# A three-stage attention and mixture-of-experts kernel: a fixed order of the last tiles and of slot 0 on all engines, kinds of slots read a slot ahead, waits per half of weights, two k pairs in most first loops

## The chip, the cores and the metric

The kernel runs on one core of one Trainium2 chip. The metric is the device time of one execution in microseconds (us); a median of three runs is given. A difference within 0.2% is about what a measurement of this kernel cannot tell from no change.

## The reference

Three stages, each feeding the next, all in float32. Cut to what is computed:

```python
def phi(x):                                   # attention features
    proj = einsum('bhsd,df->bhsf', x, w_phi)
    proj = proj - max(abs(proj), axis=-1)
    return concatenate([exp(proj), exp(-proj)], axis=-1)
q_p, k_p = phi(q), phi(k)                     # q, k, v: 8 x 8 x 576 x 64
kv = einsum('bhsf,bhsd->bhfd', k_p, v);  z = sum(k_p, axis=2)
x = einsum('bhsf,bhfd->bhsd', q_p, kv) / (einsum('bhsf,bhf->bhs', q_p, z) + 1e-06)
# x as 4608 tokens of 512
h = x @ w_in                                  # 512 x 1024
solu = h * softmax(h)
y = layernorm(solu) * g_ln @ w_out            # 1024 x 512
logits = y @ w_gate + modality_bias[modality_id]        # 8 experts
e_idx = argmax(logits);  gate = softmax(logits)[e_idx]
for e in range(8):                            # tokens of expert e
    out[e_idx == e] = gate * (maximum(y @ w1[e], 0) @ w2[e])
```

## The kernel before

**Numbers in two halves.** Products that need more than one pass are made with a high and a low part of each factor (names ending in h and l): `h` is the sum over `winh,xh`, `winl,xh` and `winh,xl`. The low part is made on DVE by subtracting the high part, which ACT has copied; the weights of an expert are split that way too, in four pieces (`w1h`/`w1l`, and `winh`/`winl`, which hold the second matrix by then).

**First stage, k pairs.** There are 32 k pairs, run by `kS`: `kA` loads `kr` and `vt_s` (SP) and makes `kps` (16 matmuls a pair), ACT and DVE make `km` and the features `kp_s`; a pair later `kv_head` (32 `kvps` matmuls) and `kM` (4 wide ones) add into `kvps`, and `kE` takes it out. 22 pairs stand in a first loop, with the steps that prepare weights (`prep_step`) between them; `RAMP` says how many pairs each of the following loops gets, ten in all with what is left for t=-1.

**Loops over tiles.** The attention outputs come in 36 chunks u, the tokens of the second stage in 36 tiles t of 128, and chunk u = t + 6 is worked on in the loop of tile t. The string `LOOP` is the order of the steps of one loop, `RLOOP` a variant for loops with one pair. For chunk u+1: `q1` makes `qps`, `qa` the maxima `mt` on DVE, `q2` the transpose `qmt`, `qb` and `qc` send the maximum through memory (`mdb`, then `mb`, both issued by SP), `q3` subtracts on DVE, `q4` makes features on ACT. For chunk u: `den`, `num`, the reciprocal through memory (`ddb`, `d`, `rb`, SP), `xm` on POOL (`x_s`), `xc` the split (`xbh` or `xh` on ACT, `xbl` or `xl` on POOL). For tile t: `m1` makes `h` (24 matmuls), `mx`, `ee` and `nrm` the softmax and the norm on ACT and DVE (`e_s`), `mT` the transposes `zT`, `zz` their split (`zh` on ACT, `zl` on DVE), `mm2` makes `y` (48 matmuls), `yc`, `ra`, `rx`, `rs`, `yo` the routing and the store; `R` makes `pos`, the place of each token in its expert's list, from `roh` (tile t) and `S` (the sum of the tiles before), and `rb` writes it with a POOL DMA (`tkb`). `XLOOP` and `TLOOP` are the loops without further chunks.

**What sets the order.** In the first part PE's order is as written and a scheduler places the other engines. From t=0 to t=30 all five engines follow the written order. In the last tiles, t=31 on (`TLOOP`, `TLOOP3`, `TAIL`), PE and POOL do; DVE, ACT and SP are placed by the scheduler, the split of slot 0's weights with a low priority.

**Slot 0.** After t=28 `star` finds the expert with the most tokens so far, and `star_w(0)` starts a 2 MB load of its first matrix on POOL's queue (`raw<-in_w`). `star_y` gathers 256 of its tokens, and `TAIL` weaves their work (`T0`, `M1`, `M2`) into tiles 33 to 35. There too `t1` to `t4` make the tables of all other slots on DVE: `cnt` (PE) counts tokens for each expert, `ctkr` is fetched by a POOL DMA, `tkT` (PE) turns it, `cidxi` are the tokens' places, `crt` the rows that the engines read. `G1` gathers the tokens of slots 1 and 2 into `yr` on POOL's queue.

**Run-time slots.** `run` works off slots of 256 tokens, j=1 to at most 24, each either full or half (up to 128 tokens). The code of slot j holds both bodies, `half` first, each under a branch on a flag; on PE a `value_load` reads the flag, then another the number of weights that must have been split (`start`). A full slot does `ph` (96 matmuls), the transposes `pT` of the next slot's tokens and `po` (48). When the expert changes, SP loads its two matrices, ACT and DVE split them, and DVE raises `sW[0]` or `sW[1]` by one when a matrix is done; PE waits for it ahead of `ph` and of `po`.

Of the kernel before, what the change touches and what calls it, by code (L numbers as in the profile page):

```python
# [7 lines left out]
F32 = mybir.dt.float32  # L8
# [17 lines left out]
RAMP = {-7: 2, -6: 2, -5: 2, -4: 2, -3: 1, -2: 1}  # L26
NOPREP = {0, 3, 6, 9, 12, 15, 18, 20}
# [75 lines left out]
class P1:  # L103
# [523 lines left out]
    def m_mm2(s, t):  # L627
# [4 lines left out]
        for j in range(2):  # L632
# [51 lines left out]
    def m_place(s, t):  # L684
# [4 lines left out]
        nc.vector.tensor_tensor(out=pe, in0=pp[:, 0:8], in1=s.cst[:, 272:280], op=ALU.add)  # L689
        nc.vector.tensor_tensor(out=pe, in0=pe, in1=oh.bitcast(F32), op=ALU.mult)  # L690
        nc.vector.tensor_reduce(out=rw, in_=pe, axis=AX.X, op=ALU.add)
        nc.vector.tensor_copy(ri, rw)
        nc.vector.tensor_tensor(out=s.S, in0=s.S.bitcast(F32), in1=oh.bitcast(F32), op=ALU.add)
        nc.gpsimd.indirect_dma_start(out=s.tk, out_offset=bass.IndirectOffsetOnAxis(ap=ri, axis=0), in_=s.cst[:, 280+t:281+t], in_offset=None, bounds_check=8*CAP-1, oob_is_err=False)

    def kS(s):
# [3 lines left out]
        if s.ga - s.gb > 1 or s.ga == NPAIR:  # L700
            s.kv_head(0)
            s.kv_head(1)
            s.kM()
            s.kE()

    def build(s, p2=None):
# [7 lines left out]
        env = dict(T=nu, ql=ok(s.q_load), q1=ok(s.q1), q2=ok(s.q2), q3=ok(s.q3), den=ok(s.q_den), num=ok(s.q_num), xm=ok(s.x_mul), xc=ok(s.x_split), m1=ok(s.m_mm1), mm2=ok(s.m_mm2), mT=ok(s.m_T), R=ok(s.m_route), rb=ok(s.m_place), nrm=ok(s.m_norm), qa=ok(s.qa), qb=ok(s.qb), yc=ok(s.m_y), ra=ok(s.m_choose), dr=ok(s.d_rec), de=ok(s.d_out), ne=ok(s.n_out), zz=ok(s.m_z), qc=ok(s.qc), q4=ok(s.q4), dl=ok(s.d_in), rx=ok(s.m_rex), rs=ok(s.m_gate), yo=ok(s.m_store), mx=ok(s.m_max), ee=ok(s.m_exp))  # L714
# [5 lines left out]
        with s.tc.manual_schedule(engines={PE}):  # L720
            s.warm(14)
            ramp = sum(RAMP.values())
            for i in range(NPAIR - ramp):
# [8 lines left out]
                if i == 20:  # L732
# [635 lines left out]
```

## Time and profile before

| | |
|---|---|
| median of 3 runs | 1348.47 us (1346.42 to 1348.48) |
| profiled execution | 1347.66 us, of which the span is 1345.5 |
| mean granted PE clock | 0.968 of full speed |
| busy | PE 96%, DVE 52%, ACT 40%, POOL 24% of the span |
| instructions | 24252 |

The span is the time from the first to the last record of the profiled execution; 2.2 us lie around it. Where PE waits, the list of waits tells which instruction waited, and by whose work the wait ended. "issue" there is a time in which PE waited for nothing that the profile shows; what its sequencer did then is to be found by the line of the program (rows whose engine ends in q: PEldq is PE's sequencer). [...]

### The profile page before, as it was taken

The page shows a single profiled execution, that of the slowest core. Times are in us where ns is not written, and L with a number is a line of the kernel's source. Part 1 is how long each engine was busy: PE and PEld are TensorE (multiplying, and loading weights), DVE is VectorE, ACT ScalarE, POOL GpSimd, SP SyncE. Part 2 cuts the span into 40 slices and gives each one's busy share as a digit, 9 for nine tenths or more (in the row PEclk, how much of TensorE's full clock was granted, in tenths as well). Part 3 has the DMA queues.
Part 4 walks back from the last instruction along what each step waited for, and adds up shares of the span by engine and source line. Part 5 has one row for each costly group of instructions (what it writes and reads, how often), then busy time and mean ns, then how long its engine had stood idle before and what let it go on. Part 6 is the DMA issues. An engine that isn't in the chain of part 4 may idle for free.

```text
span 1345.5 us, 24252 instructions
## 1 busy us (share of the span) xinstructions
PE 1285.6 (96%) x9198; PEld 1088.0 (81%) x9198; DVE 693.8 (52%) x1699; ACT 532.8 (40%) x1214; POOL 323.4 (24%) x308
## 2 busy tenths in 40 slices
PE   9999999999999999999999898989999999999994
PEld 8989788677687678777777687889899889999973
DVE  7976354477677677677677767511111141111152
ACT  5878465444344444444444423112122232212252
POOL 3644211122222222222222321121212121111121
PEclk9999599899999999999999999989999989999997
DMA  7654244135645653444345420051111141111140
GB/s 225 206 158 126 78 139 130 64 71 73 80 79 81 66 84 91 81 81 80 80 80 73 114 83 16 25 205 40 57 40 48 48 169 41 48 49 41 56 165 23
DMA packets 56425, 117.53 MB, mean 87 GB/s; under 512 B 20146, under 2 KB 20690, under 8 KB 55264
## 3 DMA queue, kind: packets, MB, share of 16 engines
q1 hardware_dynamic: 37152, 70.50, 22.6%
q10 hardware_dynamic: 10368, 18.90, 6.4%
q0 software_dynamic: 8768, 26.30, 6.0%
q8 instruction: 87, 1.43, 0.5%
q14 instruction: 50, 0.41, 0.1%
HBM read 96.16 MB, written 21.07 MB: 87 GB/s over the span
## 4 chain that ended last, share of the span: by engine, by line
PE 73%; DMA 10%; DVE 8%; issue 3%; POOL 2%; ACT 2%; SPq 1%; DVEq 0%; ACTq 0%; POOLq 0%
PE ph L869 16%; PE po L884 14%; PE y L636 11%; PE h L568 11%; DMA rb<-ddb 6%; PE kvps L373 5%; PE num L517 4%; PE qps L412 3%; PE den L475 2%; PE zT L614 2%; PE kps L314 2%; DMA ddb<-r 1%; PE pT L861 1%; DVE w1l L1241 1%; PE ph L877 1%
## 5 line engine op out<-in xcount | busy, mean ns | idle before, releaser
L899 DVE SCALAR_TENSOR_TENSOR wol<-ph,woh 128x512 fp32r<-128x512 f32 x68 | 47.0, 692 | 308.9 <-ACT woh L895 308.9
L869 PE MATMUL ph<-yh,w1h 128*128 128x256 f32 x576 | 164.7, 286 | 5.1 <-issue 2.6
L636 PE MATMUL y<-woh,zh 128*128 128x260 f32 x576 | 163.5, 284 | 0.9 <-ACT zh L623 0.9
L869 PE MATMUL ph<-yh,w1l 128*128 128x256 f32 x576 | 164.2, 285 | 0.0
L869 PE MATMUL ph<-yl,w1h 128*128 128x256 f32 x576 | 164.0, 285 | 0.0
L636 PE MATMUL y<-wol,zh 128*128 128x260 f32 x576 | 163.6, 284 | 0.0
L636 PE MATMUL y<-woh,zl 128*128 128x260 f32 x576 | 162.8, 283 | 0.2 <-DVE zl L624 0.2
L373 PE MATMUL kvps<-vt_s,kp_s 128*128 128x65 f32 x1024 | 129.6, 288 | 3.1 <-ACT kp_s L337 3.1
L373 PEld LDWEIGHTS kvps<-vt_s,kp_s 128*128 128x128 f32 x1024 | 125.0, 203 | 7.5 <-ACT kp_s L337 3.8
L884 PE MATMUL po<-winh,woh 128*128 128x512 f32 x296 | 117.1, 396 | 1.1 <-DVE wol L1318 1.1
L869 PEld LDWEIGHTS ph<-yh,w1h 128*128 128x128 f32 x576 | 111.3, 193 | 6.5 <-issue 3.0
L884 PE MATMUL po<-winh,wol 128*128 128x512 f32 x296 | 115.3, 390 | 0.0
L884 PE MATMUL po<-winl,woh 128*128 128x512 f32 x296 | 115.2, 389 | 0.0
L591 ACT ACTIVATE e_s<-h,nm 128x512 f32<-128x512 f32 x72 | 48.9, 685 | 164.7 <-DVE nm L580 152.4
L636 PEld LDWEIGHTS y<-woh,zh 128*128 128x128 f32 x576 | 109.3, 190 | 3.0 <-ACT zh L623 1.3
L869 PEld LDWEIGHTS ph<-yh,w1l 128*128 128x128 f32 x576 | 111.2, 193 | 0.6
L869 PEld LDWEIGHTS ph<-yl,w1h 128*128 128x128 f32 x576 | 111.2, 193 | 0.0
L636 PEld LDWEIGHTS y<-wol,zh 128*128 128x128 f32 x576 | 109.0, 189 | 1.4
L636 PEld LDWEIGHTS y<-woh,zl 128*128 128x128 f32 x576 | 109.2, 190 | 0.4 <-DVE zl L624 0.4
L895 ACT ACTIVATE woh<-ph 128x512 fp32r<-128x512 f32 x68 | 40.8, 600 | 158.0 <-PE ph L869 158.0
L1116 POOL DMA_INDIRECT yr<-ybuf,cidxi x42 | 45.3, 1079 | 232.2 <-ACT yh L888 221.2
L1285 ACT ACTIVATE ob<-po,gq 128x512 f32<-128x512 f32 x40 | 27.2, 687 | 168.2 <-PE po L884 168.2
(251 smaller groups left out, 2770.7 us busy)
## 6 DMA issues: line engine op xcount, KB each, us to landing
mb<-mdb SPq DMA_DIRECT2D x36, 512.0 KB
raw<-in_w SPq DMA_DIRECT2D x6, 2048.0 KB, 8.9
vt_s<-in_vi SPq DMA_DIRECT2D x32, 325.0 KB
ybuf<-ysb ACTq DMA_DIRECT2D x36, 256.5 KB
qt_s<-in_qi ACTq DMA_DIRECT2D x36, 256.0 KB
kr<-in_kt SPq DMA_DIRECT2D x36, 256.0 KB
rb<-ddb SPq DMA_DIRECT2D x72, 128.0 KB
raw<-in_win SPq DMA_DIRECT2D x8, 512.0 KB
```

The lines of the kernel that those rows point to most:

```text
L373: nc.tensor.matmul(pb[:, sg, a, :], kp[:, sg, c, :], vt[:, 4*a+c, :], start=(a == sg == c == 0), stop=False, skip_group_check=True)
L412: nc.tensor.matmul(pbs[j], s.wphi[o, :], qs[o, :], start=True, stop=True)
L517: nc.tensor.matmul(pb[64*a:64*a+64, o], s.kv[:, p // 2, 2*(p % 2) + a, sg, b, 0:64], qp[:, sg, h, c], start=(sg == 0 and (n in (0, 2))), s ...
L568: nc.tensor.matmul(h, xt(kk, a), w[:, kk, 512*j:512*j+512], start=(n == 0), stop=(n == 11))
L591: nc.scalar.activation(out=ej, in_=h[j], func=AF.Exp, bias=nm, accum_out=sums[:, j:j+1])
L636: nc.tensor.matmul(yb[j][:, 0:260], a[:, kk, :], w[:, kk, 260*j:260*j+260], start=(n == 0), stop=(n == 23))
L869: m = s.nc.tensor.matmul(ph[:, (f % 2)*256:(f % 2)*256 + 256], s.w1[w][:, k*1024 + f*128:k*1024 + f*128 + 128], x[:, k, :], start=(n == 0) ...
L884: m = s.nc.tensor.matmul(po, x[:, o*256 + h*128:o*256 + h*128 + 128], s.w2[w][:, f*512:f*512 + 512], start=(f == 0 and i == 0), stop=(f == ...
L895: return s.nc.scalar.activation(out=s.hh[:, 512*b:512*b + 512], in_=ph, func=AF.Relu)
L899: return s.nc.vector.scalar_tensor_tensor(out=s.hl[:, o], in0=ph, scalar=0.0, in1=s.hh[:, o].bitcast(F32), op0=ALU.max, op1=ALU.subtract)
L1116: G.indirect_dma_start(out=s.yr[j % 2][:, b, :], out_offset=None, in_=p.y, in_offset=bass.IndirectOffsetOnAxis(ap=idx[:, 2*j+b:2*j+b+1], a ...
L1285: A.activation(out=ob[j % 2][:, h, :], in_=po[h], func=AF.Copy, scale=s.gq[:, j % 4, h:h+1]).then_inc(sO, 1)
```

## The change

**First loops.** The first loop has 20 pairs; t=-7 to t=-3 get two each, t=-2 and t=-1 one. t=-7's loop is cut in two around the first pair's `kps`, and the last pair's `kvps` stands in t=0, between `num` and `qmt`. `xc` of chunk 4 moves to t=0. The preparation steps take two more of the early pairs.

```diff
-RAMP = {-7: 2, -6: 2, -5: 2, -4: 2, -3: 1, -2: 1}
-NOPREP = {0, 3, 6, 9, 12, 15, 18, 20}
+RAMP = {-7: 2, -6: 2, -5: 2, -4: 2, -3: 2, -2: 1, -1: 1}
+NOPREP = {0, 3, 6, 9, 12, 15}
...
-            for t in range(-1 - LEAD, -1):
+            for t in range(-1 - LEAD, 0):
                 env['t'], env['u'] = t, t + LEAD
-                do(LOOP if RAMP[t] > 1 else RLOOP)
-                for _ in range(RAMP.get(t, 0)):
-                    s.kS()
-                s.prep_step()
...
+                if t == -1 - LEAD:
+                    i = LOOP.index("q2(")
+                    do(LOOP[:i-1])
+                    s.kS(lambda: do(LOOP[i:]))
                     s.kS()
...
+                else:
+                    i = LOOP.index("mT(t)")
+                    do(LOOP[:i-1].replace("xc(u-1);", ""))
+                    s.kS()
+                    do(LOOP[i:])
...
+                if t == 0:
+                    i = LOOP.index("q2(")
+                    do(LOOP[:i-1])
+                    while s.gb < NPAIR:
+                        s.kP()
+                    do(LOOP[i:].replace("xc(u-1)", "xc(u-2);xc(u-1)").replace("ne(u)", "ne(u);kE()"))
```

PE at t=-7 before (`wT` and `wog` belong to the preparation of weights):

```order
L264 MATMUL wog<-wgt,cT 128x8 x4
L412 MATMUL qps_1586<-qt_s,wphi_s 128x512
L412 MATMUL qps_1587<-qt_s,wphi_s 128x512
L425 MATMUL qmt<-ident,mt 32x128
L314 MATMUL kps<-wphi_s,kr 128x128 x8
L373 MATMUL kvps<-vt_s,kp_s 128x65 x16
L383 MATMUL kvps<-vt_s,kp_s 128x130 x2
L314 MATMUL kps<-wphi_s,kr 128x128 x8
```

and after:

```order
L267 MATMUL wog<-wgt,cT 128x8 x4
L415 MATMUL qps_1487<-qt_s,wphi_s 128x512
L415 MATMUL qps_1488<-qt_s,wphi_s 128x512
L317 MATMUL kps<-wphi_s,kr 128x128 x8
L428 MATMUL qmt<-ident,mt 32x128
L376 MATMUL kvps<-vt_s,kp_s 128x65 x16
L386 MATMUL kvps<-vt_s,kp_s 128x130 x2
L317 MATMUL kps<-wphi_s,kr 128x128 x8
```

The `kps` of a pair, which stood behind `qmt`, now stands ahead of it.

**Last tiles.** The block of t=31 on is written out for all engines. `XLOOP` runs at t=29 and `TLOOP` at t=30, one loop earlier; `star_w(0)` comes after t=29. `split` becomes `split_a` (ACT) and `split_d` (DVE) for one piece each; two pieces of the first matrix follow t=31 and two t=32, and those of the second stand in `TAIL`. `M1` becomes `M1p` (matmuls) and `M1e` (the rest), `M2` takes a range of f; `cnt` is summed from `S` and from tile 35's `roh`; `place` hands out the steps of `rb` one by one, so that `tab1` sets its own between them; the table work is cut into `tab0`, `tab1`, `tab2`, `tab2b`, `tab3`, `tab4a`, `tab4b`, and 18 of the 24 `po` matmuls of slot 0's second half, with 6 of the first, follow `G1`.

```diff
-                do((LOOP, XLOOP, TLOOP)[max(0, t - nu + LEAD + 1)])
+                do((LOOP, XLOOP, TLOOP)[max(0, t - nu + LEAD + 2)])
...
+                if t == nu - LEAD - 1:
+                    p2.star_w(0)
...
-        with s.tc.manual_schedule(engines={PE, mybir.EngineType.Pool}):
...
-                    with s.tc.high_priority(-HP):
-                        p2.split(0)
+                if t < nu - 3:
+                    for i in range(2):
+                        p2.split_a(0, 2*(t - nu + LEAD - 1) + i)
+                    for i in range(2):
+                        p2.split_d(0, 2*(t - nu + LEAD - 1) + i)
             p2.late()
-            with s.tc.high_priority(-HP):
-                p2.split(1)
...
+TAIL = """T0();ee(T-1);mm2(T-3);SPa(1,0);SPa(1,1);SPd(1,0);nrm(T-1);yc(T-3);mT(T-2);zz(T-2);ra(T-3);rx(T-3);rs(T-3);M1p(0);M1e(0);SPa(1,2);SPd(1,1);SPa(1,3);SPd(1,2);mm2(T-2);yc(T-2)
+mT(T-1);R(T-3);zz(T-1);ra(T-2);rx(T-2);rb(T-3);rs(T-2);yo(T-3);M1p(1);R(T-2);M1e(1);rb(T-2);yo(T-2);SPd(1,3);mm2r(T-1);ycr(T-1);ra(T-1);rx(T-1);t0();R(T-1);t1(T-1);M1p(2);M1e(2);rs(T-1);yo(T-1)
+M1p(3);t2();M1e(3);t2b();M2(0,0,6);t4a();t3();G1();t4b();M2(0,6,8);M2(1,0,6);T0(1);M2(1,6,8)""".split("\n")
...
-        nc.tensor.matmul(pc[:, 0:8], p.tri[:, 128:256], p.S, start=True, stop=True)
-        n = T("cn", 8)
+        nc.tensor.matmul(pc[:, 0:8], p.tri[:, 128:256], p.S, start=True, stop=False)
+        nc.tensor.matmul(pc[:, 0:8], p.tri[:, 128:256], p.rt[t][0], start=False, stop=True)
```

DVE around tile 33's `roh` before (`lg`, `rmx`, `rec`, `rv` lead to `roh`; `winl<-raw` is a piece of the split):

```order
L655 TENSOR_SCALAR rnm<-rmx 128x1
L656 SCALAR_TENSOR_TENSOR rec<-lg,rmx,cst_s 128x8
L606 TENSOR_SCALAR e_s<-e_s,mv,va 128x1024
L657 TENSOR_TENSOR rec<-rec,cst_s 128x8
L670 TENSOR_SCALAR rse<-rse 128x1
L855 TENSOR_TENSOR winl<-raw_9186,winh 128x1024
L658 TENSOR_REDUCE rv<-rec 128x1
L671 RECIPROCAL ysb<-rse 128x1
L659 TENSOR_SCALAR roh<-rec,rv 128x8
```

and after:

```order
L885 TENSOR_TENSOR winl<-raw_9186,winh 128x1024
L609 TENSOR_SCALAR e_s<-e_s,mv,va 128x1024
L627 TENSOR_TENSOR zl<-zT,zh 128x512 x2
L657 TENSOR_TENSOR lg<-y_9681,bsel 128x8
L658 TENSOR_REDUCE rmx<-lg 128x1
L659 TENSOR_SCALAR rnm<-rmx 128x1
L660 SCALAR_TENSOR_TENSOR rec<-lg,rmx,cst_s 128x8
L661 TENSOR_TENSOR rec<-rec,cst_s 128x8
L662 TENSOR_REDUCE rv<-rec 128x1
L663 TENSOR_SCALAR roh<-rec,rv 128x8
```

The row `e_s`, which belongs to tile 35's norm, and the pieces of the split no longer stand between the steps that lead to `roh`.

**Slots.** PE reads four values of the next slot (two flags, and what `sW` must reach for each half of its weights) into registers between `pT` and `po`, or behind `ph` in a half slot; a slot begins with the branches alone. `sW` counts halves: it goes up twice for a matrix, and PE waits for the second half between the second and third quarter of `ph`, and in `po` at f=4. `crt` has an eighth column, for the second half's count. POOL gets a drain ahead of its last waits.

```diff
+            def fetch(j):
+                if j < NS:
+                    for r, z in zip(regs[j % 2], (6, 5, 0, 7)):
+                        PE.reg_load(r, rt[0:1, j, z:z+1])
+
+            def wait(z, j, i):
+                PE.wait_ge(sW[z], i + 1 if j == 1 else regs[j % 2][2+i])
+
             def start(j):
-                rg = 1 if j == 1 else load(PE, rt[0:1, j, 0:1], 1, 8)
...
             def full(j):
-                rg = start(j)
+                start(j)
                 for b in range(4):
+                    if b == 2:
+                        wait(0, j, 1)
                     s.t_mm1(ph[b], b).then_inc(sM1, 1)
                 nextT(j)
-                PE.wait_ge(sW[1], rg)
+                fetch(j + 1)
...
-                either(PE, j, full, half)
+                for x, f in zip(val[j % 2], (half, full)):
+                    with PE.If(x > 0):
+                        f(j)
+                    PE.end_ifs()
...
-                    m.then_inc(sW[z], 1)
+                        if i % 2:
+                            m.then_inc(sW[z], 1)
```

PE at the end of slot 2's code for a half slot and the start of the full one before:

```order
L884 MATMUL po_10283<-winh,wol 128x512
L1148 UNCONDITIONAL_BRANCH
L1085 TENSOR_LOAD crt
L1085 ISA x2
L1148 COMPARE_AND_BRANCH
L1085 TENSOR_LOAD crt
L1085 ISA x2
L869 MATMUL ph_10279<-yh_9718,w1h 128x256
```

and after, first behind `pT` of slot 1 and then at the same place:

```order
L891 MATMUL pT_10276<-ident,yr_9189 128x128 x4
L891 MATMUL pT_10277<-ident,yr_9189 128x128 x4
L1213 TENSOR_LOAD crt x4
L914 MATMUL po_10282<-winh,woh 128x512
L914 MATMUL po_10282<-winl,woh 128x512
```

```order
L914 MATMUL po_10282<-winh,wol 128x512
L1279 UNCONDITIONAL_BRANCH
L1279 COMPARE_AND_BRANCH
L899 MATMUL ph_10278<-yh_9645,w1h 128x256
L899 MATMUL ph_10278<-yh_9645,w1l 128x256
```

The loads of the flag and of the count, with their checks (ISA), are gone from the slot's start, and four loads stand between `pT` and `po`.

## Rows read from the trace of the kernel before

**Rows 1.** The page: busy time by engine; costliest groups (busy us, mean ns, idle before).

```profile
PE 1285.6 (96%) x9198; PEld 1088.0 (81%) x9198; DVE 693.8 (52%) x1699; ACT 532.8 (40%) x1214; POOL 323.4 (24%) x308
...
L869 PE MATMUL ph<-yh,w1h 128*128 128x256 f32 x576 | 164.7, 286 | 5.1 <-issue 2.6
```

**Rows 2.** List of waits, PE, 100 to 300 us: total, times, longest.

```profile
PE zT L614 <- DVE e_s L606: 2.8, 1, 2.8
PE qmt L425 <- DVE mt L419: 2.3, 3, 1.5
PE qps L412 <- DVE mb L447: 1.5, 1, 1.5
```

**Rows 3.** By window: length, then PE, PEld, DVE, ACT, POOL busy; PEclk, DMA share, GB/s.

```profile
142.00:166.00 24.00, 24.00 (x118) 19.83 (x119) 6.50 (x15) 11.59 (x30) 2.03 (x3) 0.50 0.21 70
...
236.00:242.00 6.00, 6.00 (x28) 1.82 (x27) 2.06 (x6) 4.43 (x13) 1.17 (x1) 0.72 0.15 48
```

**Rows 4.** Timeline of PE, 228 to 233 us: start, duration, instruction.

```profile
228.14 1.16 PE L314 MATMUL kps<-wphi_s,kr 64*128 64x128 f32 x16
229.23 3.79 PE L373 MATMUL kvps<-vt_s,kp_s 128*128 128x65 f32 x32
```

**Rows 5.** Timeline of SP, the DMA issues, 215 to 232 us.

```profile
215.27 0.33 SPq L433 DMA_DIRECT2D mdb<-qm  x1
...
217.39 0.33 SPq L439 DMA_DIRECT2D mb<-mdb  x1
...
226.49 0.47 SPq L433 DMA_DIRECT2D mdb<-qm  x1
...
231.31 0.33 SPq L439 DMA_DIRECT2D mb<-mdb  x1
```

**Rows 6.** List of waits, PE, 700 to 900 us.

```profile
PE pos L680 <- DVE roh L659: 5.2, 1, 5.2
PE h L568 <- ACT xbh L537: 3.9, 1, 3.9
PE pT L861 <- DMA yr<-ybuf,cidxi: 2.7, 2, 1.5
PE ph L869 <- DVE dm L1300: 2.5, 1, 2.5
PE zT L614 <- DVE ckey L951: 1.2, 1, 1.2
PE y L636 <- ACT zh L623: 0.9, 1, 0.9
PE h L568 <- POOL xbl L538: 0.7, 1, 0.7
```

**Rows 7.** By window, the last tiles and the slot behind a change of weights.

```profile
772.00:778.00 6.00, 5.73 (x17) 4.65 (x18) 5.13 (x12) 2.38 (x5) 0.85 (x2) 0.57 0.77 311
...
1086.00:1100.00 14.00, 14.00 (x102) 14.00 (x101) 6.26 (x7) 3.83 (x8) 0.21 (x1) 0.82 0.69 268
```

**Rows 8.** Timeline of POOL: its operation on chunk 35, with the wait ahead of it.

```profile
768.38 1.26 POOL L528 TENSOR_TENSOR x_s<-x_s,rb 128x512 f32<-128x512 f32 x1 [6.05 <-DMA rb<-ddb]
```

**Rows 9.** List of waits, PE, 900 to 1345 us.

```profile
PE ph L877 <- issue: 4.0, 1, 4.0
PE ph L869 <- issue: 2.6, 1, 2.6
```

**Rows 10.** Line 1148, PE's sequencer, at the two changes: duration ns min/median/max, first and last start.

```profile
L1148 PEldq COMPARE_BRANCH  x3: 70/985/2566, 1079.1 to 1084.0; - x3
...
L1148 PEldq COMPARE_BRANCH  x2: 65/2774/5484, 1308.2 to 1314.5; - x2
```

**Rows 11.** PE's sequencer in slots (lines 1085, 1165); PE's timeline at the last `ph`.

```profile
L1085 PEldq TENSOR_LOAD <-crt x3: 300/319/562, 903.4 to 905.4; - x3
...
L1165 PEldq EVENT_SEMAPHORE  x1: 51/51/51, 939.0 to 939.0; - x1
...
941.04 0.28 PE L869 MATMUL ph<-yl,w1h 128*128 128x256 f32 x1
```

More of the change, by code (lines that the diff above doesn't have):

```diff
@@ L625, in m_z, with m_mm2 @@
         s.z[t] = (zh, zl)
-    def m_mm2(s, t):
+    def m_mm2(s, t, order=(0, 1)):
         nc = s.nc
@@ L631, in m_mm2 @@
         yb = [s.bank(f"y{j}") for j in range(2)]
-        for j in range(2):
+        for j in order:
             n = 0
@@ L682, in m_route, with place @@
         s.rt[t] = (oh, pp)
-    def m_place(s, t):
+    def place(s, t):
         nc = s.nc
@@ L689, in m_place, with kS, kP @@
         nc.vector.tensor_tensor(out=pe, in0=pp[:, 0:8], in1=s.cst[:, 272:280], op=ALU.add)
+        yield
         nc.vector.tensor_tensor(out=pe, in0=pe, in1=oh.bitcast(F32), op=ALU.mult)
+        yield
         nc.vector.tensor_reduce(out=rw, in_=pe, axis=AX.X, op=ALU.add)
+        yield
         nc.vector.tensor_copy(ri, rw)
+        nc.gpsimd.indirect_dma_start(out=s.tk, out_offset=bass.IndirectOffsetOnAxis(ap=ri, axis=0), in_=s.cst[:, 280+t:281+t], in_offset=None, bounds_check=8*CAP-1, oob_is_err=False)
+        yield
         nc.vector.tensor_tensor(out=s.S, in0=s.S.bitcast(F32), in1=oh.bitcast(F32), op=ALU.add)
-        nc.gpsimd.indirect_dma_start(out=s.tk, out_offset=bass.IndirectOffsetOnAxis(ap=ri, axis=0), in_=s.cst[:, 280+t:281+t], in_offset=None, bounds_check=8*CAP-1, oob_is_err=False)
-    def kS(s):
+    def m_place(s, t):
+        for _ in s.place(t):
+            pass
+    def kS(s, between=None):
         s.kA(0)
         s.kA(1)
[L700 to L703, printed above, removed]
+        if between:
+            between()
+        if s.ga - s.gb > 1:
+            s.kP()
             s.kE()
+    def kP(s):
+        s.kv_head(0)
+        s.kv_head(1)
+        s.kM()
     def build(s, p2=None):
@@ L952, in tab1 @@
-        S8 = [128, 8, 8]
-        L = T("cL", 64).rearrange("p (a b) -> p a b", a=8)
-        V.tensor_tensor(out=L, in0=key[:, None, :].to_broadcast(S8), in1=key[:, :, None].to_broadcast(S8), op=ALU.is_lt)
+        place = p.place(t)
         ni = T("cni", 8, I32)
         V.tensor_scalar(out=ni, in0=n, scalar1=255.0, scalar2=None, op0=ALU.add)
+        next(place)
         V.tensor_scalar(out=ni, in0=ni, scalar1=8, scalar2=None, op0=ALU.logical_shift_right)
-        pr = T("cpr", 16).rearrange("p (a b) -> p a b", a=2)
+        next(place)
@@ L967, in tab1 @@
-        end = T("cend", 8)
+        next(place)
+        S8 = [128, 8, 8]
+        tmp = s.tmp = T("ctmp", 64).rearrange("p (a b) -> p a b", a=8)
+        st = s.st = T("cst2", 16).rearrange("p (a b) -> p a b", a=2)
+        V.tensor_tensor(out=tmp, in0=s.L, in1=pr[:, 0:1, :].to_broadcast(S8), op=ALU.mult)
+        next(place)
+        V.tensor_reduce(out=st[:, 0, :], in_=tmp, axis=AX.X, op=ALU.add)
+        next(place, None)
+        end = s.end = T("cend", 8)
         V.tensor_tensor(out=end, in0=st[:, 0, :], in1=nt, op=ALU.add)
@@ L1135, in run @@
             while_slots(G, n, gbody)
+            G.drain()
             for h in range(2):
@@ L1157, in start @@
                     PE.wait_ge(sYL, 2*j - 2)
-                PE.wait_ge(sW[0], rg)
-                return rg
+                wait(0, j, 0)
             def nextT(j):
@@ L1178, in full @@
                     for f in range(8):
+                        if h == 0 and f % 4 == 0:
+                            wait(1, j, f // 4)
                         if h == 0 and f % 2 == 0:
@@ L1184, in half @@
             def half(j):
-                rg = start(j)
+                start(j)
                 for h in range(2):
+                    if h == 1:
+                        wait(0, j, 1)
                     s.t_mm1_half(ph[h], h).then_inc(sM1, 1)
+                fetch(j + 1)
                 for h in range(2):
@@ L1199, in half @@
                     if f % 4 == 0:
+                        wait(1, j, f // 4)
                         PE.wait_ge(sHL, 4*j - 2 + f//2)
```

149 lines of the change are left out of this document (81 added, 68 removed).

## The prediction

> **What bounds the kernel now.** The page says first that TensorE (PE) is busy 1285.6 of 1345.5 us [rows 1]. So the time falls only by PE's idle spots, by work that PE did at half clock, or by less work, and the change leaves PE's arithmetic as it is. I read PE's list of waits next, for two stretches: each row gives who was waited for and how long [rows 2, 6]. The stretches by window come third, because after many of these waits the granted clock is below 1.00, and that is paid beside the wait [rows 3, 7]. For the slots the list of waits names only "issue" [rows 9]; there the rows of PE's sequencer tell what it did [rows 10, 11].
>
> **The first loops.** [...] The change (a) keeps two k pairs in all loops from t=-7 to t=-3 and puts the 16 `kps` matmuls of one pair, 1.16 us [rows 4], between `qps` and `qmt` at t=-7. The wait of 1.49 goes down to about 0.4, -1.1 (bounds 0 and -1.49), and with it goes what I take for the cause of the half clock: -12.0. (b) At t=-3 `num` and a full pair now stand where a short loop was: its `qmt` wait of 0.40 goes, the one of t=-2 stays; the three together are the 2.3 of [rows 2]. (c) At t=-1 `qps` waits 1.50, since `mdb` to `mb` took 4.82 (226.49 to 231.31) behind two `rb` transfers on the same queue, against 2.12 a loop before (215.27 to 217.39) [rows 5]. With t=-3 made longer, `rb` is out well before `mdb`: -1.50, and the 0.72 of 236 to 242 (6 x 0.28) is another -1.7 [rows 3]. (d) The last pair's `kvps` moves ahead of `qmt` and `zT(0)`; 32 such matmuls take 3.79 [rows 4], more than the 2.83 that `zT` waits: -2.83. Together -19.6.
>
> What it adds: two pairs fewer run ahead of t=-7, so SP issues one more `vt_s` load, which waits for a `kvps`, ahead of the first `mdb`. I walked that chain with the durations of the trace: `mb` lands some 4 us later, DVE's `mb` is done 1.3 us (0 to 1.8) after PE has reached `qps(1)` at t=-6, and what is queued behind on DVE is `km` of the next pair, which has slack. A wait of 1.50 brought 1.7 of slow clock [rows 2, 3], so I charge 1.3 + 1.7 = 3.0. The preparation steps that move into i=16 to 19 lie on DVE and ACT beside PE: 0 to 1, taken as 0. Net **-16.6**.
>
> [...]
>
> **The last tiles.** The order on all engines is now written out, and the 2 MB load for slot 0 goes from t=28's end to after t=29, so that it no longer runs beside `rb(35)`. What PE loses there before is: 1.2 at `zT` behind the table work of slot 0 on DVE, 3.9 and 0.7 at `h` for chunk 35, whose `x_s` waited 6.05 for `rb`, and 0.9 at `y` for `zh`, which stood behind `gq` on ACT [rows 6, 8]; 6 us at 0.57, worth 2.6 [rows 7]; 5.2 at `pos`, since `roh` was queued on DVE behind weight splits; then 2.7 at `pT` for the gather and 2.5 at slot 1's `ph` for `dm` [rows 6]. Sum 19.7. What stays or comes: `rb(35)` will land earlier than 768.38, when `x_s` began [rows 8], but POOL's two operations on it, 1.26 for the first, still stand behind its landing, and `zT` no longer holds PE back by 1.2: I leave 2.5 of the 5.8 (0 to 5.8). `pos` of tile 34 needs `S` right after tile 33's `roh`: about 1.1 (0 to 2.5). At slot 1, 24 `po` matmuls now stand between the gather and `pT`, which covers the 2.7; but `yl` and `dm` stand behind the rest of the tables on DVE, and I leave 1.7 of the 2.5 (0 to 4). The split of slot 0's weights stands in pairs ahead of `nrm` on DVE in tiles 31 and 32, where PE has little slack; 0 to 1, taken as 0, since the cover is that loop's 24 `h` matmuls. If the cover is gone, each pair costs up to its own time. Net 19.7 - 5.3: **-14.4**, between -7 and -19.7. The slow clock that follows in slot 1 I leave as it is, since some idle remains ahead of it.
>
> **The slots.** Full slots run without a gap before. PE's sequencer has the last `ph` issued and passes on at 939.0 while that matmul starts at 941.04: it leads by 2.0 us [rows 11]. Between `pT` and `po` it now does four loads of the next slot's kind and counts, at 0.300 to 0.562 each, median 0.319 [rows 11]. Four at the median with a small gap are some 1.4 us, below the lead: 0. The two loads at each slot's start go, which were hidden too. What pays is the changes of weights. At the first PE stands 2.6 [rows 9]: the sequencer did loads with their checks and three branches, of 0.070, 0.985 and 2.566 [rows 10]. Without these loads the jumps end about as the last `po` does. PE then waits for two of the four pieces of the weights' split only; for the others it waits half of `ph` later, and behind that wait nothing but `ph` itself is queued. So -2.6, and the 14 us at 0.82 that follow it [rows 7], 14 x 0.18 = 2.5, of which I take all: -5.1 (0 to -5.1). At the second, 4.0 [rows 9], a branch took 5.484 [rows 10] and remains, since the code of the two kinds keeps its place; only the loads go: -2.1 (-1 to -4). Net **-7.2**.
>
> [...]
>
> **The sum.** 16.6 + 14.4 + 7.2 = 38.2. From the profiled execution's 1347.66 (span 1345.5 and 2.2 around it) that is 1309.5. The median of the three runs lies 0.8 above the profiled one; gains that I didn't sum, the slow clock behind the 2.8 of `zT` and the 5.2 of `pos`, are about 1.7 each by the row behind the 1.50 and lie on the other side, some 2.5 in all: **1308**. The drain added on POOL stands ahead of its last waits, for scatters that end later than it: 0.
>
> **The rivals.** *A long half-clock stretch comes back*, at t=-6's wait or anywhere in i=18 to 20, where ACT is denser. For it: before, a wait of 1.49 led to 24 us of it and one of 1.50 to a few us [rows 2, 3], so the length of the wait does not decide. Against it: the first loops have fewer waits. It gives the 12.0 back: 1320. *The chains of the tail keep the gain*: DVE's tables, the gather of slot 1 and the splits ahead of `nrm` are in-order queues in which one late piece holds all. Then half of the 14.4 and half of the 7.2 go: 1308 + 10.8, some 1319, and with the first rival 1331. *Slower*: the four loads in each slot are not hidden. The point is 2.0 us: above 0.49 each (0.562 was seen once) PE idles at every slot's `po`. The idle itself is small, 0.3, but each gap can bring a stretch like 1086 to 1100, 2.5 [rows 7]. There are 576/32 = 18 full slots, 17 of them in the run-time loop [rows 1]: 17 x 2.8 = 48, which makes 1308 + 48 = 1356, slower than before. Against it: a median of 0.319, and that loads at a slot's start never held PE. *The change doesn't do what it says*: the scheduler of the first part leaves DVE and ACT as free as before, so `qmt` at t=-7 can still find `mt` late; then the 12.0 and 1.1 of (a) stay, 1321.
>
> **How the numbers follow.** The forecast, 1297 to 1315, gets 0.60. Long half clock 0.13, the tail's chains 0.12, no effect in the first part 0.06, all near or above 1319 and faster. The loads, slower, 0.06; 0.03 goes to several at once ending near the old time. The low end, 1295, takes the far bounds: 19.6 + 19.7 + 9.1 with nothing charged at t=-6, about 48, and some 4 for what I didn't sum. The high end, 1329, is the last of the faster rivals with the change's small costs. A difference within 0.2%, 2.7 us, is what a measurement of this kernel cannot tell from none. Faster 0.91, same 0.02, slower 0.07.
>
> **What would show it.** Right: the granted clock stays at 1.00 through the first loops but for a few us; `qps` at t=-6 waits about 1.3; `zT(0)` does not wait; no `pos<-roh` wait above 1; slot 1's first `ph` some 31 us earlier, about 17 of them from the first loops; no gap between full slots; the first "issue" gap gone, the second near 2. Wrong: a stretch at 0.50, waits "issue" at `po` in every slot, a wait for `e_s` in tiles 32 and 33, or `pT` still waiting for the gather.

## The result and the profile after

The changed kernel took 1320.24 us, the median of four executions (1302.93 to 1334.07), against 1348.47 before: the ratio is 0.969, 95% interval 0.964 to 0.973. It lies inside the range that was given and on its side, 12 us above the forecast and above the narrower 1297 to 1315 that had 0.60. The ratio is made from executions near each kernel's fastest, so it is not quite the ratio of the medians.

The four are two pairs: 1302.93 and 1309.41, then 1331.07 and 1334.07. The profiled execution was the 1334.07, and one row of the page separates it from another execution of the same kernel (1309.03). First the page's lines of the 1334.07: the span, and the granted clock by slice of 33 us (PEclk, in tenths of full speed).

```profile
span 1331.9 us, 24182 instructions
...
PEclk9957899999999999999999999899999999999998
```

The same of the 1309.03, with PE's busy time:

```profile
span 1306.8 us, 24182 instructions
## 1 busy us (share of the span) xinstructions
PE 1262.1 (97%) x9199; PEld 1070.4 (82%) x9199; DVE 699.8 (54%) x1700; ACT 530.6 (41%) x1214; POOL 328.3 (25%) x308
...
PEclk9999999999999999999999999899999999999998
```

PE's work is the same 9199 matmuls in both, but its busy time is 1286.9 and 1262.1. In the views by window PEclk is the granted clock as a share of full speed; of the windows of 4 us read from the 14 profiles (8 to 372, 608 to 972 and 1208 us to the end) none lies below 0.50, the lower level. By window (length, then PE, PEld, DVE, ACT, POOL busy; PEclk, DMA share, GB/s), the first execution, in the first loop:

```profile
60.00:70.00 10.00, 8.64 (x87) 8.01 (x87) 10.00 (x17) 7.46 (x20) 4.16 (x3) 1.00 0.65 202
70.00:115.00 45.00, 45.00 (x239) 43.17 (x238) 23.51 (x35) 24.46 (x66) 15.89 (x12) 0.52 0.31 99
115.00:120.00 5.00, 5.00 (x43) 4.55 (x41) 2.63 (x5) 1.74 (x4) 0.00 (x0) 0.58 0.41 119
```

and the second:

```profile
60.00:70.00 10.00, 8.65 (x87) 8.02 (x86) 10.00 (x17) 7.44 (x21) 4.16 (x3) 1.00 0.65 197
70.00:90.00 20.00, 19.77 (x190) 18.71 (x189) 17.47 (x23) 15.95 (x44) 11.91 (x9) 1.00 0.51 168
90.00:104.00 14.00, 12.49 (x88) 11.95 (x88) 7.60 (x16) 8.69 (x25) 4.39 (x4) 0.63 0.36 112
```

Up to 70 us the two agree. Then one does 45 us of unbroken work at a mean of 0.52, a loss of 45 x 0.48 = 21.6, and the other runs at full clock but for some 10 us (0.63 over the 14 from 90 on). So a single time of either kernel says little, and I split every time in two from here on. The **clock share** is (1 - mean granted clock) x span; the **rest** is the time less that share. It is an estimate, since it takes the whole span, waits with it, as if it stretched with the clock, but the rest of one kernel has a standard deviation of 1 to 3 us where its times lie up to 37 apart. (The 0.2% of the opening section came from three executions; 45 of them spread over 2.7%.) Means over the 45 executions of before that ran in the rounds of the experiments, and over the ten of after, with the 95% interval of the rest:

| kernel | executions | median us (range) | rest | clock share, mean (range) |
|---|---|---|---|---|
| before | 45 | 1346.35 (1331.85 to 1368.62) | 1306.4 ± 0.8 | 39.8 (23.9 to 64.2) |
| after | 10 | 1309.2 (1302.93 to 1334.07) | 1290.3 ± 1.6 | 25.1 (13.0 to 45.3) |

The mean went down by 30.9: 16.1 ± 1.6 in the rest, which is where waits show, and 14.7 ± 9 of clock. In the profile of the 1309.03 the span is 38.7 shorter: tile 0's first `y` starts at 248.4 instead of 266.7 (-18.3; forecast -16.6), slot 2's first `ph` at 877.55 instead of 906.58, 29.0 earlier, so the tiles gave 10.7 (14.4), and the slots 7.8 (7.2) up to PE's last matmul; 1.9 more lie behind that. As the experiments show, the first of these came out partly by luck.

PE's list of waits in the first loops of the 1309.03, from 100 us on, which answers to [rows 2] (total, times, longest):

```profile
PE qps L415 <- DVE mb L450: 1.7, 1, 1.7
PE qmt L428 <- DVE mt L422: 0.9, 2, 0.5
```

The same in the last tiles, which answers to [rows 6]:

```profile
PE tkT L1059 <- DMA ctkr<-tkb,cbi: 9.2, 1, 9.2
PE ph L899 <- DVE dm L1377: 1.8, 1, 1.8
PE pos L684 <- DVE roh L663: 0.6, 2, 0.4
PE pos L685 <- DVE rse L674: 0.4, 1, 0.4
```

And in the slots, which answers to [rows 9]:

```profile
PE po L914 <- DVE wol L1395: 1.7, 3, 1.3
PE ph L907 <- issue: 1.7, 1, 1.7
PE ph L1261 <- DVE hr L1392: 1.0, 1, 1.0
PE ph L899 <- issue: 0.7, 1, 0.7
```

The waits of [rows 2] and [rows 6] are gone or near the size forecast, and one that I gave no price has come: the 9.2 at `tkT`.

### The profile page after: what moved, and what is told of

Read it like the earlier page. It is cut to its first block, busy times and chain, and to the rows that moved or that the text cites. A ratio compares the mean times of both kernels' runs of the same rounds, so it can differ in the third digit from the quotient of the medians.

```text
span 1331.9 us, 24182 instructions
## 1 busy us (share of the span) xinstructions
PE 1286.9 (97%) x9199; PEld 1090.9 (82%) x9199; DVE 697.6 (52%) x1700; ACT 532.1 (40%) x1214; POOL 327.6 (25%) x308
## 5 line engine op out<-in xcount | busy, mean ns | idle before, releaser
L376 PE MATMUL kvps<-vt_s,kp_s 128*128 128x65 f32 x1024 | 135.8, 296 | 1.4 <-ACT kp_s L340 1.4
L376 PEld LDWEIGHTS kvps<-vt_s,kp_s 128*128 128x128 f32 x1024 | 131.2, 211 | 6.5 <-ACT kp_s L340 1.7
```

The source lines that it names most:

```text
L376: nc.tensor.matmul(pb[:, sg, a, :], kp[:, sg, c, :], vt[:, 4*a+c, :], start=(a == sg == c == 0), stop=False, skip_group_check=True)
```

## The experiments

Theory: the gain is the removed waits of three parts (first loops, last tiles, slots), and the half clock follows a particular wait, the 1.49 at t=-7. Rival: the half clock comes by chance after any of several short idles, and the first loops gave less than the first profile says. In the tail, theory: `tkT` waits because three scatters run in series. Ratios are to before in the same runs, with 95% intervals.

**The changed kernel once more.**

```diff
(no edit)
```

> The changed kernel itself, once more. Theory: its times fall into two groups, because the stretch at half clock in the first loops (70 to 118 us in its first profile, 0.52 and 0.58) comes in some executions and not in others, from the same program and the same short waits before it. Then some times lie near 1303 to 1310 and some near 1331 to 1334, about 24 us apart, and a profile of the low group shows no stretch at 0.50 longer than 10 us before 240 us. Rival: the stretch belongs to the change and is always there; the low times come from elsewhere, such as the tail, and a profile of the low group still shows it.

Measured: 1307.83 (1304.25 to 1327.68), ratio 0.973 (0.966 to 0.980). Both groups of times appear again: 1304 to 1309 and 1324 to 1328. Of the ten executions four lie above 1320.

**The first loops alone**, and **all but the first loops**.

```diff
 (before)
-RAMP = {-7: 2, -6: 2, -5: 2, -4: 2, -3: 1, -2: 1}
+RAMP = {-7: 2, -6: 2, -5: 2, -4: 2, -3: 2, -2: 1, -1: 1}
...
```

> The kernel before with the change of the first loops alone. Theory: the first loops are worth 24 us where the half clock stays away (up to the first matmul of tile 0's y: 266.7 us before, 266.3 after, of which the stretch cost 23.7) and nothing where it comes: times near 1324 and near 1348, in two groups. Rival, my prediction's form: the edit takes the cause of the half clock away, the times are one group near 1348 - 16.6 = 1332.

```diff
 (after)
-RAMP = {-7: 2, -6: 2, -5: 2, -4: 2, -3: 2, -2: 1, -1: 1}
+RAMP = {-7: 2, -6: 2, -5: 2, -4: 2, -3: 1, -2: 1}
...
```

> The changed kernel with the first loops of the kernel before. Theory: what lies behind the first loops gives 13.2 (from tile 0's y to the end 1078.8 us before, 1065.6 after), so near 1335; and if the half clock of the old first loops sits behind the 1.49 wait in each execution, the times lie within 4 us of each other, as those of the kernel before do. Rival: the half clock is a matter of chance here too, then two groups some 12 us apart. By my prediction's terms, 14.4 + 7.2, it would be 1327.

Measured: 1330.74 (1323.12 to 1347.99), ratio 0.991 (0.987 to 0.996), and 1325.76 (1316.10 to 1344.38), ratio 0.985 (0.979 to 0.992). Neither run has the two groups that were expected of the one, or the 4 us of spread that were expected of the other. The rest is 1300.9 ± 1.9 with the first loops alone and 1294.2 ± 2.6 without them: they are worth 5.5 added to before, and 3.9 taken from after. The clock share falls by 9.1 ± 6 with them and rises by 7.5 ± 13 without. So the part is worth some 11 to 15 in the mean (3.9 + 7.5 to 5.5 + 9.1), and clock is the larger part of it by these means, though the second of them is not clear of nothing.

**The slots alone.**

```diff
 (before)
+                        PE.reg_load(r, rt[0:1, j, z:z+1])
...
-                either(PE, j, full, half)
+                for x, f in zip(val[j % 2], (half, full)):
...
-                    m.then_inc(sW[z], 1)
+                        if i % 2:
+                            m.then_inc(sW[z], 1)
```

> The kernel before with the change of the slots alone. Theory from the trace: from slot 2 to the end of PE 423.9 us before and 420.6 after, so -3.4, and some 1.8 at the end: near 1344. Prediction: -7.2, 1341. Rival: the four loads in each slot cost something that the shorter first loops hide in no way: above 1348.

Measured: 1340.75 (1328.19 to 1353.89), ratio 0.998 (0.994 to 1.002), rest 1302.1 ± 1.8, that is -4.3. By times alone this would be "no effect"; the rest, which the clock does not cover up, finds it. The loads cost nothing, as forecast: line 1213, PE's sequencer, over the slots of the 1309.03 of after (duration ns min/median/max, first and last start), and no wait in front of a `po` that they end.

```profile
L1213 PEldq TENSOR_LOAD <-crt x72: 295/300/485, 864.6 to 1250.8; - x72
```

This run also bears on the half clock at t=-7. Its first loops are those of before, 1.49 wait included. By window:

```profile
104.00:136.00 32.00, 32.00 (x310) 30.77 (x311) 19.17 (x37) 28.13 (x72) 15.34 (x13) 1.00 0.39 115
136.00:168.00 32.00, 30.51 (x286) 25.51 (x282) 18.89 (x41) 22.01 (x50) 6.30 (x6) 1.00 0.47 147
```

The idle is there (32 - 30.51 = 1.49), and the clock stays at 1.00, where before ran 24 us at 0.50 [rows 3]. Its tile 0 starts at 252.5, 14.2 earlier than in the profile of before, with nothing changed ahead of it. So 14 of the 18.3 above are to be had by chance. But the wait is not without effect: with the first loops undone, behind the same 1.49 at 154.09, the stretch is there again, and so is the one behind pair 10:

```profile
154.09 0.27 PE L428 MATMUL qmt<-ident,mt 128*32 128x128 f32 x1 [1.49 <-DVE mt L422]
```

```profile
70.00:115.00 45.00, 45.00 (x243) 43.03 (x241) 23.92 (x36) 24.84 (x67) 15.87 (x12) 0.53 0.31 99
...
154.00:178.00 24.00, 23.91 (x121) 22.25 (x121) 7.06 (x16) 8.85 (x22) 4.22 (x4) 0.51 0.24 82
```

Over the profiles without the dummy matmuls of the next experiment, the 1.49 at t=-7 was followed by such a stretch in two of the three that have it, and the 1.01 of pair 10 in three of ten. In the seven with the changed first loops nothing longer than some 7 us follows at t=-7 (a loss of 3.4 at most).

**Filling the idle spots of the first loops**, in before and in after. Matmuls of no use, whose results are overwritten, stand where PE waits for `kp_s` in three pairs, and ahead of `qmt` at t=-7 (six in before, two in after).

```diff
+            for _ in range({9: 1, 10: 4, 14: 6}.get(s.gb, 0)):
+                nc.tensor.matmul(s.kvps[s.gb][:, 0:128], s.wphi, s.wphi, start=True, stop=True)
...
+        if u == 0:
+            for _ in range(6):
+                nc.tensor.matmul(tp[:, 0:128], s.wphi, s.wphi, start=True, stop=True)
```

> The kernel before with idle matmuls on a constant tile, whose result is overwritten, in four places where PE waits in the first loops (pairs 9, 10, 14: 1, 4 and 6; ahead of `qmt` at t=-7: 6), so that PE has work in the waits of 0.34, 1.01, 1.50 and 1.49 us. If a short idle is what lets the clock fall, then no profile or run has the long stretches at 70 to 120 and 138 to 168 us, the mean clock is above 0.975 in every run, and the median falls by some 12 to 15 us from the 1345 of before, the time less the clock's share staying at 1307. Rival: what the stretches need is not idle but the work of the first loops as such, and chance; then the mean clock spreads as before, 0.953 to 0.981.

> The same filling in the changed kernel (pairs 9, 10, 14: 1, 4, 6; ahead of `qmt` at t=-7: 2). If idle lets the clock fall: the upper group near 1324 to 1334 is gone, all runs 1303 to 1310 and the mean clock 0.985 or more. Rival: the spread stays, 1303 to 1334.

Measured: before with fillers 1328.34 (1326.10 to 1333.55), ratio 0.988 (0.984 to 0.991), clock share 21.2 to 26.6; after with fillers 1307.02 (1305.42 to 1310.45), ratio 0.971 (0.968 to 0.975), clock share 11.7 to 15.7. The range shrinks from 37 us to 7, and from 31 to 5. By window, before with fillers:

```profile
70.00:90.00 20.00, 19.77 (x189) 18.71 (x190) 19.81 (x28) 17.84 (x48) 15.45 (x12) 1.00 0.63 186
90.00:104.00 14.00, 14.00 (x146) 13.32 (x148) 11.12 (x20) 12.08 (x32) 6.62 (x6) 1.00 0.49 156
104.00:136.00 32.00, 32.00 (x305) 30.00 (x305) 18.03 (x36) 26.74 (x68) 10.74 (x10) 1.00 0.38 113
136.00:168.00 32.00, 32.00 (x299) 25.66 (x295) 18.68 (x37) 22.96 (x57) 6.30 (x7) 1.00 0.45 134
```

The fillers at one of the spots, PE's timeline of after with fillers; the wait of up to 1.5 ahead of `kvps` is covered:

```profile
90.01 1.16 PE L317 MATMUL kps<-wphi_s,kr 64*128 64x128 f32 x16
91.10 1.60 PE L373 MATMUL kvps<-wphi_s 128*128 128x128 f32 x12
92.55 3.68 PE L378 MATMUL kvps<-vt_s,kp_s 128*128 128x65 f32 x32
```

So in the profiles without the idle at these spots the long stretches did not come, and with it they came in some executions and not in others; what decides between them no run shows. Not every idle brought one: the fillers leave the 2.8 at `zT` in before, and it is followed by some 3 us at the lower level (240 to 250 us at 0.83), and the 8.6 at `tkT` in after by some 10 (830 to 860 us at 0.83). Whether the k pairs that follow the two spots make the difference was not tried. Of 24 executions of after, of the earlier route and of the full slot first (both below) 7 lie above 1320; of 18 with fillers none. In before the fillers act on the clock alone: its rest with them is 1305.6 ± 3.0, as without. That of after is 1293.5 ± 1.8, some 3 more than without, which stays unexplained.

**The tail: the route of tile 33 earlier.** In after the three scatters of `tkb` for tiles 33 to 35 and the gather `ctkr` follow one another on POOL's queue (timeline of POOL, the 1309.03):

```profile
816.22 1.03 POOL L700 DMA_INDIRECT tkb<-cst_s,rri  x1 [12.70 <-DVE rse L674]
823.10 0.97 POOL L700 DMA_INDIRECT tkb<-cst_s,rri  x1 [5.85 <-DVE rpe L693]
831.24 0.98 POOL L700 DMA_INDIRECT tkb<-cst_s,rri  x1 [7.17 <-DVE cpad L1053]
839.38 1.03 POOL L1044 DMA_INDIRECT ctkr<-tkb,cbi  x1 [7.16 <-DMA tkb<-cst_s,rri]
```

6.9, 8.1 and 8.1 from one issue to the next. Each was issued behind the landing of the one before: in the 1334.07 the three scatters landed 6.4, 7.1 and 6.8 after their issue, and what followed was issued 7.1, 7.9 and 7.7 after it. (For the second and third the trace names a DVE step, but their row numbers, `rri`, are done at 817.6 and 823.7, over 5 us before they are issued; for `ctkr` it names the scatter itself.) The experiment sets `pos` and the store of tile 33 into tile 34's `y`.

```diff
-...SPd(1,2);mm2(T-2);yc(T-2)
-mT(T-1);R(T-3);zz(T-1);ra(T-2);rx(T-2);rb(T-3);rs(T-2);...
+...SPd(1,2);mm2m(T-2);rb(T-3);yc(T-2)
+mT(T-1);zz(T-1);ra(T-2);rx(T-2);rs(T-2);...
```

> The changed kernel with the place of tile 33 worked out one step earlier: its two `pos` matmuls stand between the halves of tile 34's y, and DVE's steps behind the last two weight pieces. Theory: in the tail PE waits 8.7 us for `ctkr`, because the three `tkb` scatters of tiles 33 to 35 (issued at 837.8, 844.95 and 852.8, each only when the one before has landed, 6.4 to 7.2 us later) stand in a row ahead of it. Begun some 5.5 us earlier, the chain ends 5 to 6 us earlier: the wait for `ctkr` falls to 2 to 4 us, and the time less the clock's share ((1 - mean clock) x span; 1290.5 for the changed kernel) to about 1285. Rival: the wait hangs on `blkT` and the tables on DVE; then it stays at 8 to 9 us and the time is the same.

Measured: 1305.90 (1302.16 to 1311.58), ratio 0.970 (0.967 to 0.973); the wait is

```profile
PE tkT L1061 <- DMA ctkr<-tkb,cbi: 5.4, 1, 5.4
```

3.8 shorter, so the series is the cause, but not as short as expected: the three now stand at 814.02, 820.97 and 829.30, `ctkr` at 838.46, and the last step took 9.2 instead of 8.1. (PE is 3.1 later here, by `pT` of slot 0 at 798.4 and 795.3, so against PE the first scatter is 5.3 earlier and `ctkr` 4.0.) The first step no longer looks held by a landing either. The second scatter is issued right behind its own row numbers, which DVE has done at 820.69:

```profile
820.97 1.78 POOL L702 DMA_INDIRECT tkb<-cst_s,rri  x1 [5.92 <-DVE rri L701]
```

So an earlier start for tile 33 alone cannot bring the chain forward by its whole amount; tile 34's places come next. The rest, 1290.3 ± 2.6, does not show the gain; what is seen in the trace is below its interval or lost elsewhere.

**The load for slot 0 back behind t=28**, and **`XLOOP` back at t=30**, each alone, to see which of the two edits took the waits at `h` away.

```diff
 (after)
                     p2.star()
+                    p2.star_w(0)
...
-                if t == nu - LEAD - 1:
-                    p2.star_w(0)
```

> The changed kernel with the 2 MB load of slot 0's first matrix back behind t=28, where it stood. Theory: it then runs beside `rb(35)`, which takes 10 to 13 us instead of the 3.6 of the changed kernel, and PE waits 3 to 5 us for chunk 35 at `h` of tile 30. Rival: the earlier XLOOP made the room; PE waits 0 to 1.

```diff
 (after)
-                do((LOOP, XLOOP, TLOOP)[max(0, t - nu + LEAD + 2)])
+                do((LOOP, XLOOP, TLOOP)[max(0, t - nu + LEAD + 1)])
```

> The changed kernel with XLOOP and TLOOP back at t=30 and t=31's order, the load staying behind t=29. Theory: the load is what held `rb(35)`; with it out of the way PE waits at most 1 us at `h` of tile 30 with either loop. Rival: without the earlier XLOOP POOL's work for chunk 35 comes late and PE waits 2 to 4 us.

Measured, one execution each: 1313.33 and 1315.03. PE's waits with the load early,

```profile
PE h L571 <- ACT xbh L540: 2.0, 1, 2.0
...
PE h L571 <- POOL xbl L541: 1.7, 1, 1.7
```

and POOL's wait for chunk 35's `rb`, first with the load early, then in after:

```profile
741.78 1.26 POOL L531 TENSOR_TENSOR x_s<-x_s,rb 128x512 f32<-128x512 f32 x1 [8.48 <-DMA rb<-ddb]
```

```profile
741.01 1.29 POOL L531 TENSOR_TENSOR x_s<-x_s,rb 128x512 f32<-128x512 f32 x1 [4.15 <-DMA rb<-ddb]
```

With `XLOOP` late PE does not wait at `h`, but at `zT` of tile 30. The list names `lg`, which runs beside it (748.29 to 748.44); what the transposes read is `e_s`, whose norm DVE ends at 748.36, and `zT` starts at 748.51 (list of waits, then DVE's timeline):

```profile
PE zT L617 <- DVE lg L657: 2.2, 1, 2.2
```

```profile
746.61 1.75 DVE L609 TENSOR_SCALAR e_s<-e_s,mv,va 128x1024 f32<-128x1024 f32 x1 [0.69 <-POOL va L604]
```

The table work of slot 0 had ended at 732.90. In `TLOOP`, which after has at t=30, 12 matmuls of `h` stand between the start of the norm and `zT` and cover it; with `XLOOP` there, nothing does. So, by one execution each, the later load takes the transfer out of `rb`'s way, 3.7 at PE, and the earlier `XLOOP` and `TLOOP` cover tile 30's norm, 2.2. Each does a part that the other doesn't.

**The code of the full slot ahead of that of the half slot**, for the branches at the changes of weights.

```diff
-                    for r, z in zip(regs[j % 2], (6, 5, 0, 7)):
+                    for r, z in zip(regs[j % 2], (5, 6, 0, 7)):
...
-                for x, f in zip(val[j % 2], (half, full)):
+                for x, f in zip(val[j % 2], (full, half)):
```

> The changed kernel with the two bodies of a slot in the other order on PE, full before half. [...] With full first it runs on from the half slot into the full one without a jump, and both gaps go (0.38 + 2.35, and up to 2 us of slow clock): the time less the clock's share falls from 1290.5 to about 1288. Rival: the 2.35 belongs to the weights' second half or to the loads; then the gap stays. If the jump over a half body between full slots were not hidden any more, there would be gaps in other slots.

The 0.38 and the 2.35 are PE's idle ahead of `ph` at the first change of the 1334.07, up to 1074.28 and 1077.35; ahead of the first lies a branch of 3.51, which PE's sequencer began at 1070.2. For the second the trace names no releaser:

```profile
1077.35 0.28 PE L899 MATMUL ph<-yh,w1l 128*128 128x256 f32 x1 [2.35 <-issue]
```

Measured: 1316.24 (1306.46 to 1327.28), ratio 0.977 (0.971 to 0.983), rest 1290.1 ± 3.1: no difference clear of that interval. PE's "issue" waits at the two changes, from the lists of all profiles:

| slots | first change | second change |
|---|---|---|
| as before (3 profiles) | 2.6, 2.3, 2.2 | 4.0, 3.9, 2.2 |
| new, half ahead (9) | 2.7, 0.7, 1.2, 3.0, 2.3, 0, 0, 1.7, 0.7 | 0.9, 1.7, 2.2, 2.0, 0.8, 2.3, 1.0, 2.2, 0.8 |
| new, full ahead (2) | 0, 0 | 2.8, 0.6 |

In the two profiles with 0 and half ahead, PE waits 1.2 and 1.1 for `w1l` there instead. With the full slot ahead the first gap is gone in both profiles, and no such wait comes; but it is 0 to 3.0 without that edit, so two profiles don't show that the order does it. The second stays open, at 0.6 and 2.8. The branch there took 5.99 with the full code ahead, and 5.15 in the 1309.03 of after (line 1279, PE's sequencer, second change). Two half slots meet there, and in either order one full body lies between them, so the two orders do not differ there:

```profile
L1279 PEldq COMPARE_BRANCH  x2: 65/2608/5151, 1274.5 to 1279.9; - x2
```

**All together**: fillers, the route of tile 33 some matmuls earlier still, and eight fillers ahead of `tkT`; the second with the full slot ahead too.

```diff
+                    if mid and j == order[0] and n == 10:
+                        mid()
...
         pb = p.bank("tkT")
+        for _ in range(8):
+            nc.tensor.matmul(pb[:, 0:128], p.ident, p.ident, start=True, stop=True)
```

> The changed kernel with the filling of the first loops as in the run of the changed kernel, the place of tile 33 worked out earlier still (its `pos` inside the first half of tile 34's y, DVE's steps ahead of the last two weight pieces, tile 34's routing ahead of tile 35's `zl`), and eight idle matmuls ahead of `tkT` in the wait for `ctkr`. Theory: the chain of three scatters starts some 3 us earlier than with the first shift, the wait for `ctkr` is 2 to 4 us instead of 5.4, part of it filled; the clock's share is 9 to 14 us in each run. Median near 1300 and all runs within 1296 to 1306. Rival: the chain is held by the landing of the scatters alone, which takes longer when they come closer together, and the median stays at 1305 to 1307.

> The same with the full body ahead of the half body on PE. [...] Rival: the gap of the first change is the larger one and this order is 3 us faster.

Measured: 1302.32 (1298.09 to 1306.70), ratio 0.971 (0.965 to 0.976), and 1301.81 (1300.16 to 1304.66), ratio 0.971 (0.965 to 0.976). `tkT` waits 3.9 and 3.0, behind 2.0 of fillers: from the start of the fillers to `tkT` it is 5.9 and 5.0, against a wait of 5.4 with the first shift, so the still earlier start brought little or nothing. Its second scatter, too, is issued right behind tile 34's own row numbers (done at 814.71, issued at 814.99, 9.3 after the first, in the first of the two). The medians are 7 below the 1309.2 of after, but that is clock (share 12.1 and 11.3, against 25.1): the rest is 1290.1 ± 1.6 and 1290.7 ± 0.9, that of after. Against after with fillers it is 3 lower; since the route alone gained nothing, neither that 3 nor the 3 that the fillers seemed to cost is settled. The order of the two bodies makes no difference that is clear of these intervals, and the rival's 3 us did not come. The expected 1296 to 1306 is met but for one execution. What both bring is that no execution is above 1306.7, where after reaches 1334.07.

## Why the prediction was right, and where it was not

**The first loops: the waits were right, the price of the clock was not.** Waits at `qmt` and `zT(0)` went as worked out; `qps` at t=-6 waits 1.7 in the 1309.03 and 1.3 in most other profiles (1.3 forecast). The waits of the part summed to -4.5 net, and the rest measured -5.5 added and -3.9 taken away. (The terms of the -19.6 add up to 19.5.) The step that failed is "with it goes what I take for the cause of the half clock: -12.0". The 12.0 is half of the 24.00 us of work at 0.50 in [rows 3], and that stretch was one draw of a chance: the same wait brought one again with the first loops undone and none of it in the run of the slots alone. So the wait did go, and its stretch with it, but 12.0 was the price of an execution that has it, not of all. And the 1.01 us wait of pair 10, which the change leaves, brought some 47 us of it in after (45 at 0.52 and 5 at 0.58) and nothing in before; my list of waits began at 100 us, and that wait lies at 69 (PE's timeline, first before, then after; the last bracket is the idle ahead):

```profile
69.32 3.79 PE L373 MATMUL kvps<-vt_s,kp_s 128*128 128x65 f32 x32 [1.01 <-ACT kp_s L337]
```

```profile
69.18 5.14 PE L376 MATMUL kvps<-vt_s,kp_s 128*128 128x65 f32 x32 [1.01 <-ACT kp_s L340]
```

Over many executions the clock share of the whole kernel fell by 14.7 ± 9, close to the 17 of my terms, which is why the sum held; that closeness is partly luck, since it is a mean over a wide spread, and I wrote it as a certain amount of one place. The rival "a long half-clock stretch comes back" had 0.13; times above 1320, which are its mark, came in 4 of 10 executions, and in 7 of the 24 above. It is also the first of my signs of being wrong, and the profiled execution shows it. The 1320.24 on record is the middle of two of each kind; that the rival gave 1320 is an accident, for its stretch would have cost 12 and this one cost some 24.

Unbroken work did not soon end a stretch: 45.00 us of it ran at 0.52 in the 1334.07, after the 24.00 at 0.50 in [rows 3]. What makes the spread of 1331.85 to 1368.62 in one kernel no run shows, but with such a spread I should have given that rival more than 0.13.

**The last tiles: two steps off, in opposite directions.** `pos` waits 1.0 in all (1.1 forecast), `dm` 1.8 (1.7), `pT` nothing, `zT` 0.2. Slot 1's first `ph` stands 26.5 earlier (31 forecast). Where I left 2.5 for chunk 35, nothing is left: `x_s` still waits 4.15 for `rb`, but PE doesn't wait at `h`. And the `ctkr` gather, to which I gave no price, costs 9.2 at `tkT` (8.7 and 7.3 in the two runs with one edit taken back). I had followed the gather of slot 1 and DVE's tables, and not the three scatters ahead of it on POOL's queue, since no such row stands in [rows 6]. The 1.2 at `zT`, too, I had put down to table work, since the list names `ckey`; as in the run with `XLOOP` late it was tile 30's norm, which ends at 763.17, and `zT` starts at 763.32 (DVE, before):

```profile
762.36 0.81 DVE L606 TENSOR_SCALAR e_s<-e_s,mv,va 128x1024 f32<-128x1024 f32 x1 [0.69 <-POOL va L601]
```

By the lists, the 17.1 of waits that I summed became 12.0, a gain of 5.1. In the rest, last tiles and slots together are 1306.4 - 1294.2 = 12.2, of which the slots have 4.3, so the last tiles 7.9 ± 3; my terms without clock were 4.7 for the slots and 11.8 for the tiles. The tail's waits are the term that was mis-sized, by some 4 to 7.

**The slots: the size was right, one row of it wrong.** The loads are hidden (median 0.300, 72 of them), so the slower rival had no ground. I took all of the first change's 2.6 as gone; nine profiles have 0 to 3.0 there, on average 1.4. The second was given 1.9 and has 1.5 on average, 0.8 to 2.3. At the first change the branch takes 3.51 in the 1334.07 of after, about the 0.985 and 2.566 of [rows 10] together, and in the 1309.03 no branch is longer than 0.449:

```profile
L1279 PEldq COMPARE_BRANCH  x3: 70/226/449, 1049.5 to 1050.3; - x3
```

So taking the loads out did not make the branch short; it differs between executions of one kernel, 0.449 and 3.51, and why was not tried. The step "without these loads the jumps end about as the last `po` does" holds in some executions only.

## What to carry to other kernels

Before a stretch of half clock is priced as the effect of one wait, look whether the same wait brings it in other executions; if only in some, price it as a chance of that wait, look for other short idles in the same stretch of work, and give the time as two groups. Split every time into a clock share and a rest before small parts are compared: a part worth 4 us was invisible in times that spread by 25 and plain in the rest. When waits in front of a chain are removed, walk every queue that the chain passes, DMA queues with their landings too: the next wait, 9.2 at `tkT`, was three transfers that the waits taken out had covered. And where the list of waits names a releaser, look at what the waiting instruction reads: here it named a neighbour of the true one more than once.

## What was not expected of the hardware

- PE stayed at a mean clock of 0.52 through 45.00 us of unbroken work, after an idle of 1.01 us that brought no such stretch in seven of ten profiles. In the four profiles with dummy matmuls in the idle spots (22 instructions ahead of `kvps` in all, some 3 us at the 1.60 for 12 shown above) no window from 60 to 120 us lies below 1.00, and over their 24 executions the clock share is 21.2 to 26.6 in before and 9.1 to 17.0 in after.
- A compare-and-branch on PE took 0.065 us, and 5.15 at the same line where it leads over the other body of the slot (1309.03, second change); at the first change the longest took 3.51 in one execution of a kernel and 0.449 in another.
- Indirect scatters to one table, each behind the landing of the one before, were issued 6.9 to 8.3 us apart, and the gather behind them 7.7 to 9.2 after the last, in four profiles of after and its variants. In the 1309.03 it is 23.2 us from the first scatter to the gather.
